# A fused attention and MLP kernel on one core: hand-written instruction order replaced by a list schedule with a timing model

## The chip, the cores and the metric

The kernel runs on one core of one Trainium2 chip. The metric is device time in microseconds (us) of one execution, lower is better. Runs of one kernel mostly agree within about 1%; times below are medians of runs in the fast state, also where record and table of a kernel include a slow one. Engines are named as in the profile: PE is TensorE, PEld its weight loads, DVE is VectorE, ACT is ScalarE, POOL is GpSimd, SP is the queue that issues most transfers.

## The reference

Squared-ReLU attention without softmax, followed by a squared-ReLU MLP. Inputs and output are float32.

```python
batch, n_heads, seq, head_dim = (8, 12, 448, 64)     # q, k, v
n_tokens, d_model, d_ff = (3584, 768, 2048)          # w_in, w_out

scores = scale * np.matmul(q, k.transpose(0, 1, 3, 2))
attn = np.maximum(scores, 0.0) ** 2 / S
attn_out = np.matmul(attn, v)
x = attn_out.transpose(0, 2, 1, 3).reshape(B * S, H * D)
h = x @ w_in
r = np.maximum(h, 0.0)
out = (r * r) @ w_out
```

## The kernel before

All matmuls are fp16. PE has five kinds of work. Scores go to `sp` and attention times values to `avt`, both as groups of four 64x64 matmuls. The first layer goes to `hps`. The second layer goes to `ops`; most of it is a seven-product scheme in place of eight, which needs sums of activations that DVE makes into `comb`. Twelve transposes of q and k are the fifth kind.

Squared ReLU is done in two halves on two engines. For scores, DVE takes the maximum and ACT squares, or ACT takes the ReLU and POOL multiplies. For the first layer, ACT squares and DVE multiplies by the mask `x > 0`:

```python
def relu2(ps, dst, scale):
    nc.scalar.activation(out=dst, in_=ps, func=AF.Square, scale=scale)
    nc.vector.scalar_tensor_tensor(
        out=dst, in0=ps, scalar=0.0, in1=dst, op0=ALU.is_gt, op1=ALU.mult)

def by_sbuf(ps, dst, r, scale, first):
    if first is nc.vector:
        nc.vector.tensor_scalar_max(r, ps, 0.0)
        return lambda: nc.scalar.activation(out=dst, in_=r, func=AF.Square, scale=scale)
    nc.scalar.activation(out=r, in_=ps, func=AF.Relu, scale=scale)
    return lambda: nc.gpsimd.tensor_mul(dst, r, r)
```

The order on every engine is the order in which the program calls these. After a start of its own, the program goes in "bursts": two tiles of scores, their squared ReLU, perhaps the 28 matmuls of attention times values, then a share of dense work (first and second layer) from a queue:

```python
def soft_burst(g, pool):
    todo = []
    for z, (n, t, sp) in enumerate(g):
        ...                                    # cut: buffers
        if z == 1 and not pool:
            relu2(ps, at, SK)
        else:
            todo.append(by_sbuf(ps, at, r, SK, nc.scalar if z else nc.vector))
    for fn in todo:
        fn()

for i in range(STREAM // 2, NB):
    ...                                        # cut: scores of two tiles into g
    soft_burst(g, not 22 < i <= 30)
    ...                                        # cut: attention x values, new dense work, loads
    run_some(max(0.0, (queued - KEEP) / (nxt - i)))     # dense work
```

Of the kernel before, what the change touches and what calls it, by code (L numbers as in the profile page):

```python
# [12 lines left out]
ALU = mybir.AluOpType  # L13


@with_exitstack
def kernel(
# [23 lines left out]
    NF = FF // P  # L41
    HALF = DM // 2
# [5 lines left out]
    ctx.enter_context(tc.manual_schedule())  # L48

    const_p = ctx.enter_context(tc.tile_pool(name="const", bufs=1))  # L50
    v_p = ctx.enter_context(tc.tile_pool(name="vp", bufs=4))
    raw_p = ctx.enter_context(tc.tile_pool(name="rawp", bufs=2))
    blk_p = ctx.enter_context(tc.tile_pool(name="blkp", bufs=2))
    qkt_p = ctx.enter_context(tc.tile_pool(name="qktp", bufs=3))
    at_p = ctx.enter_context(tc.tile_pool(name="atp", bufs=12))
    x_p = ctx.enter_context(tc.tile_pool(name="xp", bufs=2))
    g_p = ctx.enter_context(tc.tile_pool(name="gp", bufs=2))
    rest_p = ctx.enter_context(tc.tile_pool(name="restp", bufs=2))
    comb_p = ctx.enter_context(tc.tile_pool(name="combp", bufs=6))
    part_p = ctx.enter_context(tc.tile_pool(name="partp", bufs=6))  # L60
    rel_p = ctx.enter_context(tc.tile_pool(name="widep", bufs=2))

    PSUM = bass.MemoryType.PSUM
    s_p = ctx.enter_context(tc.tile_pool(name="sps", bufs=2, space=PSUM))
    mm_p = ctx.enter_context(tc.tile_pool(name="mmps", bufs=4, space=PSUM))






    raw: dict = {}
    early: list = []
    blk: dict = {}
    qkt: dict = {}
    vst: dict = {}

    def load_qk(n, w, eng, gate=None):
        b, u = divmod(n, NU)
        if n in (1, 2):  # L80
            if not early:
                early.append(g_p.tile([P, 4, 2 * TJ * D], FP32, name="early", tag="g"))
            t = early[0][:, 2 * n - 2 + (w == "k")].rearrange("p (f x) -> p f x", f=2)
        else:
            t = raw_p.tile([P, 2, TJ * D], FP32, name=w + "f", tag=w + "f")
        if gate is not None:
            gate.memset(t[0:1, 0, 0:1], 0.0)
        src = q if w == "q" else k
        eng.dma_start(
            out=t,  # L90
            in_=src[b, 4 * u:4 * u + 4].rearrange(
                "(f e) (p t) d -> (e p) f (t d)", e=2, t=TJ))
        raw[n, w] = t

    def cast_qk(n, w, op):
        src = raw.pop((n, w))
        t = blk_p.tile([P, TJ, 2 * D], FP16, name=w + "s", tag=w + "s")
        op(t.rearrange("p t (f d) -> p f t d", f=2),
           src.rearrange("p f (t d) -> p f t d", d=D))
        blk[n, w] = t  # L100

    def turn_dma(n, w):
        t = qkt_p.tile([P, TJ, P], FP16, name=w + "T", tag=w + "T")
        nc.sync.dma_start_transpose(
            out=t, in_=blk.pop((n, w)).rearrange("p t c -> p (t c)"))
        qkt[n, w] = t

    def turn_pe(n, w, op):
        src = blk.pop((n, w))
        ps = mm_p.tile([P, TJ * P], FP16, name="tps", tag="mm")  # L110
        for t in range(TJ):
            nc.tensor.transpose(ps[:, t * P:(t + 1) * P], src[:, t, :], ident)
        t = qkt_p.tile([P, TJ, P], FP16, name=w + "T", tag=w + "T")
        op(t.rearrange("p t c -> p (t c)"), ps)
        qkt[n, w] = t

    def load_v(n):
        b, u = divmod(n, NU)
        t = vst[n] = v_p.tile([P, 2, TJ * D], FP16, name="vs", tag="vs")
        src = v[b].rearrange("(u x) (p t) d -> p u x (t d)", x=4, t=TJ)  # L120
        for r in range(2):
            hs = slice(1, 3) if r else slice(0, 4, 3)
            nc.gpsimd.dma_start(out=t[64 * r:64 * r + 64], in_=src[:, u, hs])  # L123

    w1 = [const_p.tile([P, NM, 512], FP16, name=f"w1_{i}", tag=f"w1_{i}") for i in range(4)]
    w2 = [[const_p.tile([P, NF // 2, HALF], FP16, name=f"w2_{hf}{i}", tag=f"w2_{hf}{i}")
           for i in range(2)] for hf in range(2)]

    def load_w1(i):
        nc.gpsimd.dma_start(  # L130
            out=w1[i],
            in_=moe_w_in[:, 512 * i:512 * (i + 1)].rearrange("(m p) f -> p m f", p=P))

    def load_w2(hf, i):
        nc.gpsimd.dma_start(
            out=w2[hf][i],
            in_=moe_w_out[1024 * i:1024 * (i + 1), hf * HALF:(hf + 1) * HALF].rearrange(
                "(f p) d -> p f d", p=P))

    NH = NF // 2  # L140
    LO, HI = slice(0, HALF), slice(HALF, DM)
    wt = [const_p.tile([P, NH, HALF], FP16, name=f"wt_{i}", tag=f"wt_{i}") for i in (1, 2, 4)]
    t1, t2, t4 = wt

    def combine_w2(k, eng):
        step, r = k // 2, slice(4 * (k % 2), 4 * (k % 2) + 4)
        (b11, b21), (b12, b22) = w2
        if step == 0:
            eng.tensor_sub(t1[:, r], b12[:, r], b11[:, r])
        elif step == 1:  # L150
            eng.tensor_sub(t2[:, r], b22[:, r], t1[:, r])
        elif step == 2:
            eng.tensor_sub(t4[:, r], t2[:, r], b21[:, r])
        else:
            eng.tensor_sub(b12[:, r], b22[:, r], b12[:, r])


    fifo: deque = deque()
    queued = 0.0
    xts: dict = {}  # L160
    gts: dict = {}
# [7 lines left out]
    credit = 0.0  # L169

    def run_some(ns):
        nonlocal queued, credit
        credit += ns
        while fifo and credit > 0:
            c, fn = fifo.popleft()
            fn()
            queued -= c
            credit -= c

    def relu2(ps, dst, scale):  # L180
        nc.scalar.activation(out=dst, in_=ps, func=AF.Square, scale=scale)  # L181
        nc.vector.scalar_tensor_tensor(  # L182
            out=dst, in0=ps, scalar=0.0, in1=dst, op0=ALU.is_gt, op1=ALU.mult)

    def by_sbuf(ps, dst, r, scale, first):

        if first is nc.vector:
            nc.vector.tensor_scalar_max(r, ps, 0.0)  # L188
            return lambda: nc.scalar.activation(out=dst, in_=r, func=AF.Square, scale=scale)  # L189
        nc.scalar.activation(out=r, in_=ps, func=AF.Relu, scale=scale)  # L190
        return lambda: nc.gpsimd.tensor_mul(dst, r, r)  # L191

    PARTS = slice(0, 4 * TP), slice(4 * TP, S)
    WHOLE = slice(0, S)

    def h_pair(f, cols):

        if 0 not in gts:
            gts[0] = g_p.tile([P, NF, S], FP16, name="g", tag="g")
        cell = [None]  # L200
        w = cols.stop - cols.start

        def half(z):
            def run():
                if z == 0:
                    cell[0] = mm_p.tile([P, 512], FP32, name="hps", tag="mm")
                for m in range(NM):
                    nc.tensor.matmul(  # L208
                        cell[0][:, z * w:z * w + w],
                        lhsT=w1[(f + z) // 4][:, m, (f + z) % 4 * P:((f + z) % 4 + 1) * P],  # L210
                        rhs=xts[0][:, m, cols], start=(m == 0), stop=(m == NM - 1),
                        skip_group_check=True)
                if z == 1:
                    relu2(cell[0][:, 0:2 * w].rearrange("p (f c) -> p f c", c=w),
                          gts[0][:, f:f + 2, cols], 1.0)
            return run

        return [(0.422 * w * NM, half(z)) for z in range(2)]

    def h_groups(b):  # L220
        gt = gts[b] = g_p.tile([P, NF, S], FP16, name="g", tag="g")
        xt = xts[b]

        def group(f):
            def run():
                hps = mm_p.tile([P, 512], FP32, name="hps", tag="mm")
                for m in range(NM):
                    nc.tensor.matmul(  # L228
                        hps[:, 0:S],
                        lhsT=w1[f // 4][:, m, (f % 4) * P:(f % 4 + 1) * P],  # L230
                        rhs=xt[:, m, :], start=(m == 0), stop=(m == NM - 1))
                relu2(hps[:, 0:S], gt[:, f, :], 1.0)
            return run

        return [(189.0 * NM, group(f)) for f in range(NF)]

    def store(places, cols, osb):
        for i, (b, t) in enumerate(places):
            nc.sync.dma_start(
                out=out[b * S:(b + 1) * S, cols].rearrange(  # L240
                    "(p t) d -> p t d", t=TJ)[:, t, :],
                in_=osb[64 * i:64 * i + 64])
# [178 lines left out]





    ats: dict = {}

# [271 lines left out]
```

## Time and profile before

| | before |
|---|---|
| time, median of 2 runs | 441.63 us (440.77 to 442.5) |
| span of the profiled run, mean granted clock | 436.3 us, 0.976 |
| all matmuls at the pace of runs without a wait | 344.3 us |
| steps between 64x64 and 128x128 work (176 of about 95 ns) | 16.6 us |
| PE not getting on ("stalls"): before 80 us, 80 to 380 us, after | 28.8, 39.1, 1.1 us |

Rows three to five are worked out from the start times of the matmuls in the trace. Within an undisturbed run a 448-column matmul starts 189 ns after the one in front of it, a 384-column one 163 ns, a round of four 64x64 ones about 188 ns; what two starts lie further apart, less 95 ns where the size of the array tile changes, is counted as a stall, in the stretch in which it begins. Start and tail are the other 6.5 us. Half-clock time is inside the stalls: about 20 us of the span have half the clock, so at most about 10 us of the stalls are due to it.

The page of the kernel before gives each engine's busy time, its share of the span and its instructions, and, further down, the chain of work that ended last by engine:

```profile
PE 388.4 (89%) x3264; PEld 204.4 (47%) x3264; DVE 272.7 (63%) x367; ACT 253.1 (58%) x383; POOL 231.1 (53%) x200
...
PE 53%; DVE 24%; ACT 16%; issue 6%; POOL 0%; DVEq 0%; ACTq 0%
```

PE is nearly always busy by this count, and yet only 53% of the chain runs over PE: for 40% of the span it was DVE or ACT that set the time. The view of waits of before says who waited for whom (total us, times, longest); these are lines on DVE, ACT and PE:

```profile
DVE g L182 <- ACT g L181: 94.1, 86, 2.5
ACT at L189 <- DVE rel L188: 78.0, 67, 6.2
...
PE sp L438 <- DVE rel L188: 9.3, 10, 2.9
...
PE avt L494 <- DVE g L182: 5.3, 10, 1.0
```

The first two lines together are a loop between ACT and DVE. The timeline of before shows one turn of it (start, us, engine, line, operation, and in brackets the idle time in front and who ended it):

```profile
285.44 3.58 PE L228 MATMUL hps<-xt,w 128*128 128x448 f16 x18
...
286.09 0.92 ACT L190 ACTIVATE rel<-sp 128x896 f32<-128x896 f32 x1
...
286.87 1.08 DVE L188 TENSOR_SCALAR rel<-sp 128x896 f32<-128x896 f32 x1
...
287.99 0.95 ACT L189 ACTIVATE at<-rel 128x896 f16<-128x896 f32 x1 [0.98 <-DVE rel L188]
288.84 1.39 ACT L181 ACTIVATE g<-hps 128x448 f16<-128x448 f32 x3
...
289.40 1.69 DVE L182 SCALAR_TENSOR_TENSOR g<-hps,g 128x448 f16<-128x448 f32 x3 [1.45 <-ACT g L181]
290.08 0.35 PE L494 MATMUL avt<-at,vs 64*64 64x448 f16 x1 [0.56 <-DVE g L182]
...
291.00 1.08 DVE L188 TENSOR_SCALAR rel<-sp 128x896 f32<-128x896 f32 x1
```

Three groups of six first-layer matmuls start at 285.44 us; at 189 ns each the first group is through at about 286.6. ACT could square it from 287.01 on, but the next operation in ACT's queue is the square `at`, whose input DVE finishes only at 287.95. ACT stands 0.98 us with work behind it that is ready. So the three squares of `g` come at 288.84, DVE stands 1.45 us in front of the masks, PE runs out of buffers and waits, and the next `rel` on DVE comes late, after which the loop begins again. The Trainium skill (TensorE: Matmul & The Clock Gate, section "Architectural detail: the array is 16× 32×32, not 1× 128×128") says that "ACT/DVE are strict FIFO"; the trace agrees in this place. It is not so in each of the 67 waits of the second line above. In the trace, a 448-column square of the first layer follows the start of its sixth matmul by 0.39 us at the least; by this measure such a square was ready behind the waiting score square in 26 of the 67 waits, for 18 of the 78.0 us. In the other waits no such square was held up.

### The profile page before, as it was taken

The numbers are of one execution on the slowest core, as the hardware profiler recorded it, in microseconds if no ns is written. First come the engines' busy times: TensorE is split into PE (matmuls) and PEld (weight loads), VectorE is DVE, ScalarE is ACT, GpSimd is POOL, SyncE is SP. The second block draws the span as 40 slices with busy tenths as digits, with TensorE's granted clock in tenths as the row PEclk, the third lists the DMA queues.
The fourth block names the chain that finished last, engine by engine and source line by source line (L and its number), as shares of the span: only waits on it lengthen the run. The fifth ranks groups of instructions, "written<-read, shape, count | busy, mean of one in ns | idle before, by whom it ended". The sixth has DMA issues, their size and how long they took to land.

```text
span 436.3 us, 8172 instructions
## 1 busy us (share of the span) xinstructions
PE 388.4 (89%) x3264; PEld 204.4 (47%) x3264; DVE 272.7 (63%) x367; ACT 253.1 (58%) x383; POOL 231.1 (53%) x200
## 2 busy tenths in 40 slices
PE   7688887899889999999899899997769997999995
PEld 3455655444445444444454444543434443555563
DVE  4756556378985558565875765764596654645642
ACT  3676578667645775577457476666526675434121
POOL 4768367999935575476746465564275433200100
PEclk9869989999989999999999999999998999999999
DMA  8999995886066464686176274656053200220143
GB/s 276 171 260 226 252 220 90 231 201 144 0 147 133 126 113 116 154 165 155 31 201 153 59 168 71 162 137 148 8 111 80 54 2 2 72 56 0 46 97 75
DMA packets 69669, 53.61 MB, mean 123 GB/s; under 512 B 36864, under 2 KB 69632, under 8 KB 69632
## 3 DMA queue, kind: packets, MB, share of 16 engines
q1 hardware_dynamic: 55152, 40.84, 36.3%
q0 software_dynamic: 14208, 11.80, 18.2%
q8 instruction: 25, 0.41, 0.4%
q10 hardware_dynamic: 272, 0.46, 0.3%
q14 instruction: 12, 0.10, 0.1%
HBM read 45.61 MB, written 11.01 MB: 130 GB/s over the span
## 4 chain that ended last, share of the span: by engine, by line
PE 53%; DVE 24%; ACT 16%; issue 6%; POOL 0%; DVEq 0%; ACTq 0%
PE ops L302 23%; PE hps L228 15%; DVE rel L188 11%; ACT at L189 8%; DVE g L182 6%; ACT g L181 5%; PE avt L494 5%; PE sp L438 4%; DVE comb L283 4%; PE ops L266 2%; PE hps L208 2%; PE warm L565 1%; ACT xt L509 1%; DVE osb L313 1%; ACT rel L190 1%
## 5 line engine op out<-in xcount | busy, mean ns | idle before, releaser
L191 POOL TENSOR_TENSOR at<-rel 128x896 f16<-128x896 f32 (+2 forms) x70 | 118.5, 1693 | 141.2 <-ACT rel L190 140.8
L228 PE MATMUL hps<-xt,w 128*128 128x448 f16 x672 | 136.4, 353 | 7.9 <-DVE g L182 4.4
L182 DVE SCALAR_TENSOR_TENSOR g<-hps,g 128x448 f16<-128x448 f32 (+2 forms) x128 | 76.5, 621 | 94.3 <-ACT g L181 94.1
L189 ACT ACTIVATE at<-rel 128x896 f16<-128x896 f32 (+4 forms) x91 | 85.7, 943 | 78.6 <-DVE rel L188 78.0
L188 DVE TENSOR_SCALAR rel<-sp 128x896 f32<-128x896 f32 (+4 forms) x91 | 97.5, 1073 | 16.9 <-PE sp L438 14.8
L228 PEld LDWEIGHTS <-w 128*128 128x128 f16 x672 | 62.9, 98 | 75.8 <-issue 22.4
L181 ACT ACTIVATE g<-hps 128x448 f16<-128x448 f32 (+2 forms) x128 | 65.1, 537 | 32.4 <-PE hps L228 28.2
L190 ACT ACTIVATE rel<-sp 128x896 f32<-128x896 f32 (+2 forms) x70 | 64.1, 915 | 16.4 <-PE sp L438 15.0
L438 PE MATMUL sp<-qT,kT 64*64 64x448 f16 (+2 forms) x756 | 53.6, 349 | 15.2 <-DVE rel L188 9.3
L302 PEld LDWEIGHTS <-comb 128*128 128x128 f16 x416 | 40.1, 100 | 40.3 <-issue 9.6
L494 PE MATMUL avt<-at,vs 64*64 64x448 f16 (+2 forms) x756 | 45.0, 338 | 10.0 <-DVE g L182 5.3
L313 DVE SCALAR_TENSOR_TENSOR osb<-ops,part 128x384 f32<-128x384 f32 x52 | 28.6, 553 | 37.6 <-ACT part L308 30.7
L308 ACT ACTIVATE part<-ops 128x384 f32<-128x384 f32 x52 | 24.8, 486 | 34.6 <-PE ops L302 33.7
L302 PE MATMUL ops<-wt,comb 128*128 128x384 f16 x208 | 38.5, 337 | 4.9 <-DVE comb L283 4.7
L302 PE MATMUL ops<-w,comb 128*128 128x384 f16 x208 | 38.0, 334 | 2.0 <-ACT part L308 2.0
L438 PEld LDWEIGHTS <-kT 64*64 64x64 f16 x756 | 17.2, 107 | 45.0 <-issue 43.6
L494 PEld LDWEIGHTS <-vs 64*64 64x64 f16 x756 | 25.2, 109 | 24.5 <-issue 17.5
L302 PEld LDWEIGHTS <-g 128*128 128x128 f16 x264 | 25.3, 98 | 18.9 <-issue 2.5
L302 PE MATMUL ops<-w,g 128*128 128x384 f16 x176 | 30.9, 326 | 0.0
L123 POOL DMA_DIRECT2D vs<-in_v_dram x48 | 30.0, 630 | 0.1
L283 DVE TENSOR_TENSOR comb<-g 128x1024 f16<-128x1024 f16 x22 | 25.9, 1176 | 0.1
L208 PE MATMUL hps<-xt,w 128*128 128x256 f16 (+1 forms) x192 | 24.7, 278 | 0.8 <-DVE g L182 0.4
(49 smaller groups left out, 255.2 us busy)
## 6 DMA issues: line engine op xcount, KB each, us to landing
out_dram<-osb SPq DMA_DIRECT2D x112, 96.0 KB, 2.2
kf<-in_k_dram SPq DMA_DIRECT2D x22, 448.0 KB, 4.1
qf<-in_q_dram SPq DMA_DIRECT2D x21, 448.0 KB, 4.8
vs<-in_v_dram POOLq DMA_DIRECT2D x48, 112.0 KB, 3.1
w<-in_moe_w_in_dram POOLq DMA_DIRECT2D x4, 768.0 KB, 15.7
w<-in_moe_w_out_dram POOLq DMA_DIRECT2D x4, 768.0 KB, 18.2
early<-in_k_dram SPq DMA_DIRECT2D x2, 448.0 KB, 7.2
early<-in_q_dram SPq DMA_DIRECT2D x2, 448.0 KB, 8.1
```

Of the source, the lines that this page charges most:

```text
L181: nc.scalar.activation(out=dst, in_=ps, func=AF.Square, scale=scale)
L182: nc.vector.scalar_tensor_tensor(out=dst, in0=ps, scalar=0.0, in1=dst, op0=ALU.is_gt, op1=ALU.mult)
L188: nc.vector.tensor_scalar_max(r, ps, 0.0)
L189: return lambda: nc.scalar.activation(out=dst, in_=r, func=AF.Square, scale=scale)
L190: nc.scalar.activation(out=r, in_=ps, func=AF.Relu, scale=scale)
L191: return lambda: nc.gpsimd.tensor_mul(dst, r, r)
L208: nc.tensor.matmul(cell[0][:, z * w:z * w + w], lhsT=w1[(f + z) // 4][:, m, (f + z) % 4 * P:((f + z) % 4 + 1) * P], rhs=xts[0][:, m, cols] ...
L228: nc.tensor.matmul(hps[:, 0:S], lhsT=w1[f // 4][:, m, (f % 4) * P:(f % 4 + 1) * P], rhs=xt[:, m, :], start=(m == 0), stop=(m == NM - 1))
L283: op(t, x, y)
L302: nc.tensor.matmul(st[bank][:, 0:HALF], lhsT=st[a][:, j, :], rhs=w(j), start=(first and j == 0), stop=(j == NH - 1), skip_group_check=True)
L438: nc.tensor.matmul(sp[64 * c:64 * c + 64, e, at:at + w].rearrange("p (t c) -> p t c", c=TP), lhsT=kT[r, t, 64 * e:64 * e + 64], rhs=qT[r, ...
L494: nc.tensor.matmul(ap[f][64 * e:64 * e + 64, at0:at0 + w], lhsT=vs[r, e ^ c, t * D:(t + 1) * D], rhs=at[r, e, :], start=(t == 0), stop=(t ...
```

## The change

The intent is to let a small simulation choose the order. While the program is built, every operation is added to a `Plan` with its duration, its inputs, its buffers and a due time. An event loop then plays the program: whenever an engine is free it takes, of the operations that are ready and have buffers, the one with the earliest due time. The engine of an elementwise operation can be left open (ACT or DVE, ACT or POOL), and the buffer is whichever is free. What the loop issues is emitted in that order; the result is a fixed program, nothing is decided on the chip. The number of matmuls and the transfers are as before, and so is the arithmetic, except that eight score tiles which were squared and then masked are now treated like the others. Buffers that were bound to one use or engine are now drawn from common pools. The core of the diff:

```diff
+class Plan:
+    LAG = {"PE": 0.22, "ACT": 0.07, "DVE": 0.07, "POOL": 0.1, "SP": 0.0}
+    SWITCH = {("dense", "tile"): 0.09, ("tile", "dense"): 0.235}
...
+    def run(self):
...
+            now = heapq.heappop(events)
...
+                for eng in ("PE", "ACT", "DVE", "POOL", "SP"):
+                    if self.busy[eng] > now + 1e-9:
+                        continue
+                    got = self.pick(eng, now, waiting)
...
+                    op.end = begin + took
+                    self.busy[eng] = begin + busy
...
+                    emit()
...
+    def pick(self, eng, now, waiting):
+        for z, (_, _, op) in enumerate(waiting):       # sorted by due time
+            if op.ready > now + 1e-9:
+                continue
+            for alt in op.alts:
+                if alt[0] != eng:
+                    continue
+                if len(alt) > 5 and self.busy["POOL"] > now + 0.4 and op.due > now:
+                    continue
...                                                     # cut: are buffers free?
+                    return z, alt
...
+    def square(op, sp, width, pool="at"):
...
+        first = plan.add([
+            dve(n, lambda: nc.vector.tensor_scalar(...)),
+            act(n, lambda: nc.scalar.activation(...))],
+            [op], [sp, r], due=plan.now + 0.2)
+        second = plan.add([
+            act(n, lambda: nc.scalar.activation(out=dst(), in_=rel(), func=AF.Square)),
+            ("POOL", 0.0018 * n + 0.05, 0.0018 * n + 0.08,
+             lambda: nc.gpsimd.tensor_mul(dst(), rel(), rel()))],
+            [first], [r, at], due=plan.now + 4.0)
...
-        soft_burst(g, not 22 < i <= 30)
...
+            second, at = square(op, sp, S)
...
+    plan.run()
```

## The prediction

> **What bounds the kernel now.** TensorE. The page gives PE 89% busy, DVE 63%, ACT 58%, POOL 53%. From the start times of matmuls I get the pace inside a run without waits: 189 ns per 448-column matmul of the first layer, 163 ns per 384-column matmul of the second, about 188 ns per round of four 64x64 matmuls. At that pace all matmuls together need about 344 us. Steps between 64x64 and 128x128 work cost about 95 ns each over the pace, 176 times: 17 us. Start and tail are 6.5 us. The rest of the 436.3 us span, about 69 us, is PE not getting on: 29 us before 80 us, 39 us from 80 to 380 us, 1 us after that (the chain of waits there is matmuls alone). About 10 us of the 69 are clock: the granted clock is 0.976 on average, with half-clock stretches mostly before 68 us, some at 132 and 337 us. The Trainium skill (TensorE: Matmul & The Clock Gate, Part 1) describes a half-rate state after idle windows; the records agree (only 1.0 and 0.5 occur).
>
> The waits name the cause: score matmuls wait for DVE or ACT to empty the two score buffers (19 big gaps, about 18 us by starts), attention-value matmuls, 21 gaps, 14 us, first layer 22, 13 us, second layer 24, 10 us. No engine that serves PE is full. These are order losses: in the chain, PE stands behind `rel` (11%) and `at` (8%) while dense work is ready but later in its fixed order. DVE sums (`comb`) take 0.68 us undisturbed, 1.1 on average and once 5.0 us with POOL active at the same time (window 312 to 332 us: PE waited 2.9 us after that).
>
> **What the change does.** The arithmetic, matmul count, shapes and stores stay. PE floor 344 us and the number of mode steps stay about the same. Moved: PE takes the earliest-due ready operation; evacuations go to whichever of ACT, DVE, POOL the model finds free (rel 1.08 us on DVE or 0.92 on ACT, square 0.95 on ACT or 1.69 on POOL); sums wait for a quiet POOL and are placed 7 us ahead. Elementwise work (DVE 273, ACT 253, POOL 231 us) fits easily under 400 us. Its constants (0.1892, 0.1625, 0.00081 and 0.001045 us per element, 3.06 us POOL subtraction) match this trace. Costs: order is still static, so wrong times become head-of-line waits; SP queue order mixes loads, transposes and stores.
>
> **Sum (estimates from the numbers above).** 80 to 380 us: of 35 us of stalls other than clock, a little over half goes, -20. Before 80 us: DMA is 80 to 90% busy there and clock is cold, so only -6. Tail 0; mode steps +2. About -24 us.
>
> Predicted 417 us, 80% range 402 to 434. Faster by over 2%: 0.72; within: 0.17; slower: 0.11.
>
> **Checks in the profile.** PE busy share rises to about 93%; matmul sum unchanged; stalls by starts fall from 69 to about 45 us; waits of scores on `rel` shrink most; `comb` mean falls toward 0.7 to 0.8 us; POOL/ACT/DVE busy totals within 10%; the first 80 us shorten by about 6 us; PE mode steps about 176.
>
> **What would make it wrong.** Model time drifting from chip time, so that engines block on operations placed too early; POOL and DVE colliding more; loads or transposes queued late behind stores on SP; greedy PE order multiplying mode steps; the first 80 us limited by transfers.

## The result, and the profile after

After takes 397.24 us (median of 2 runs, 396.36 to 398.11) against 441.63 us. The ratio is 0.8995, with a 95% interval of 0.8881 to 0.9109. A ratio is the mean time of one kernel's fast runs over that of the other's fast runs of the same rounds, so it is not quite the ratio of the medians. The prediction said faster, which was right, but 417 us with a range from 402, which was not: the gain is 44 us, not 24.

| | before | after |
|---|---|---|
| profiled span, clock | 436.3 us, 0.976 | 396.3 us, 0.983 |
| matmuls at their pace | 344.3 us | 344.1 us |
| steps between 64x64 and 128x128 work | 176, 16.6 us | 184, 17.3 us |
| stalls before 80 us | 28.8 us | 20.5 us |
| stalls 80 to 380 us | 39.1 us | 7.8 us |
| stalls after 380 us | 1.1 us | 0.0 us |

The sum of the differences is the whole of the 40 us between the two spans: the stalls went, and little else moved. (The profiled run of before was the fastest of its kind, 438.1 us, that of after the slower of two, hence 40 rather than 44.) The page of after, the same two lines:

```profile
PE 377.3 (95%) x3264; PEld 200.3 (51%) x3264; DVE 264.7 (67%) x364; ACT 268.8 (68%) x392; POOL 222.4 (56%) x194
...
PE 80%; DVE 7%; POOL 4%; DMA 3%; ACT 3%; issue 2%; SPq 0%; DVEq 0%; POOLq 0%; ACTq 0%
```

The chain now runs over PE for 80% of the span. The waits of after (line numbers differ: L456 is the mask, L461 the first-layer square, L381 the score square on ACT, L383 that on POOL, L374 the maximum on DVE, L348 the scores):

```profile
POOL at L383 <- DVE rel L374: 75.3, 35, 6.6
DVE g L456 <- ACT g L461: 48.9, 67, 2.2
...
ACT at L381 <- DVE rel L374: 5.5, 6, 2.3
...
PE sp L348 <- DVE rel L374: 2.1, 4, 1.0
```

The wait of the score square on ACT fell from 78.0 to 5.5 us, that of the mask from 94.1 to 48.9. A part of the first fall is only a change of engine: POOL now squares tiles that DVE emptied, which before was left to ACT, and has the wait for them (75.3 us). The timeline of after, in a stretch like the one above:

```profile
228.77 0.57 PE L348 MATMUL sp<-qkt,qkt 64*64 64x448 f16 x8
228.88 0.54 ACT L461 ACTIVATE g<-mm 128x448 f16<-128x448 f32 x1 [0.64 <-PE mm L472]
...
229.28 2.44 PE L472 MATMUL mm<-xt,w 128*128 128x448 f16 x12
229.32 0.91 ACT L377 ACTIVATE rel<-sp 128x896 f32<-128x896 f32 x1
229.47 1.09 DVE L374 TENSOR_SCALAR rel<-sp 128x896 f32<-128x896 f32 x1 [1.29 <-PE sp L348]
230.26 0.95 ACT L381 ACTIVATE at<-rel 128x896 f16<-128x896 f32 x1
230.48 0.61 DVE L456 SCALAR_TENSOR_TENSOR g<-mm,g 128x448 f16<-128x448 f32 x1
230.64 1.68 POOL L383 TENSOR_TENSOR at<-rel 128x896 f16<-128x896 f32 x1 [0.76 <-DVE rel L374]
```

ACT, DVE and POOL wait here only for something that PE or DVE has just made, and PE has no wait at all.

The start is different. The first score matmul began at 8.07 us before and begins at 12.20 us after. In the timeline of after, DVE at the start:

```profile
8.50 0.62 DVE L291 COPY qkt<-mm 128x896 f16<-128x896 f16 x1 [7.35 <-PE mm L288]
...
9.04 0.62 DVE L271 CAST blk<-raw 128x896 f16<-128x896 f32 x1
```

The cast at 9.04 is that of the very first q, which ACT loads; before, its cast began at 5.80. The plan lets ACT issue that load only at 2.6 us and so reckons that it lands at 10.0 us, after both loads of the next unit, and puts a copy for that unit in front of it.

### The profile page after: what moved, and what is told of

The parts are those of the page before. It is cut to its first block, busy times and chain, and to the rows that moved or that the text cites. A ratio compares the mean times of both kernels' runs of the same rounds, so it can differ in the third digit from the quotient of the medians.

```text
span 396.3 us, 8280 instructions
## 1 busy us (share of the span) xinstructions
PE 377.3 (95%) x3264; PEld 200.3 (51%) x3264; DVE 264.7 (67%) x364; ACT 268.8 (68%) x392; POOL 222.4 (56%) x194
## 4 chain that ended last, share of the span: by engine, by line
PE 80%; DVE 7%; POOL 4%; DMA 3%; ACT 3%; issue 2%; SPq 0%; DVEq 0%; POOLq 0%; ACTq 0%
PE mm L472 34%; PE mm L623 26%; PE sp L348 9%; PE mm L411 8%; DVE comb L602 3%; PE mm L561 3%; DVE rel L374 2%; DMA g<-in_q_dram 2%; POOL at L383 2%; DMA raw<-in_q_dram 1%; POOL blk L271 1%; DVE g L456 1%; PE mm L288 1%; ACT rel L377 1%; POOL wt L587 1%
## 5 line engine op out<-in xcount | busy, mean ns | idle before, releaser
L472 PE MATMUL mm<-xt,w 128*128 128x448 f16 (+2 forms) x864 | 157.3, 332 | 0.3 <-DVE g L456 0.3
L383 POOL TENSOR_TENSOR at<-rel 128x896 f16<-128x896 f32 (+1 forms) x60 | 102.3, 1705 | 86.7 <-DVE rel L374 75.3
L374 DVE TENSOR_SCALAR rel<-sp 128x896 f32<-128x896 f32 (+2 forms) x88 | 94.2, 1073 | 36.8 <-PE sp L348 29.3
L456 DVE SCALAR_TENSOR_TENSOR g<-mm,g 128x448 f16<-128x448 f32 (+2 forms) x128 | 79.2, 620 | 49.3 <-ACT g L461 48.9
L461 ACT ACTIVATE g<-mm 128x448 f16<-128x448 f32 (+2 forms) x128 | 68.9, 541 | 45.7 <-PE mm L472 44.0
L381 ACT ACTIVATE at<-rel 128x896 f16<-128x896 f32 (+2 forms) x98 | 91.1, 940 | 9.2 <-DVE rel L374 5.5
L348 PE MATMUL sp<-qkt,qkt 64*64 64x448 f16 (+2 forms) x756 | 52.4, 353 | 4.7 <-DVE rel L374 2.1
L271 POOL CAST blk<-raw 128x896 f16<-128x896 f32 x42 | 39.8, 957 | 22.3 <-issue 7.7
L545 ACT ACTIVATE part<-mm 128x384 f32<-128x384 f32 x48 | 23.5, 489 | 41.0 <-PE mm L623 38.9
L623 PE MATMUL mm<-wt,comb 128*128 128x384 f16 x208 | 37.0, 327 | 1.4 <-DVE comb L602 1.4
L411 PE MATMUL mm<-at,vs 64*64 64x448 f16 (+1 forms) x672 | 37.3, 339 | 0.4 <-POOL at L383 0.4
L623 PEld LDWEIGHTS <-g 128*128 128x128 f16 x264 | 24.8, 98 | 20.1 <-issue 4.3
L348 PEld LDWEIGHTS <-qkt 64*64 64x64 f16 x756 | 17.3, 110 | 30.8 <-issue 30.2
L317 POOL DMA_DIRECT2D vs<-in_v_dram x48 | 30.1, 633 | 0.1
```

What stands on the lines that cost most here:

```text
L271: return lambda: fn(blk.tile.rearrange("p t (f d) -> p f t d", f=2), tile_of().rearrange("p f (t d) -> p f t d", d=D))
L317: nc.gpsimd.dma_start(out=buf.tile[64 * r:64 * r + 64], in_=src[:, u, hs])
L348: nc.tensor.matmul(sp[64 * c:64 * c + 64, e, c0:c0 + w].rearrange("p (t c) -> p t c", c=TP), lhsT=kT[r, t, 64 * e:64 * e + 64], rhs=qT[r, ...
L374: dve(n, lambda: nc.vector.tensor_scalar(out=rel(), in0=sp.tile[:, :, 0:width], scalar1=0.0, scalar2=SK, op0=ALU.max, op1=ALU.mult)),
L381: act(n, lambda: nc.scalar.activation(out=dst(), in_=rel(), func=AF.Square)),
L383: lambda: nc.gpsimd.tensor_mul(dst(), rel(), rel()))],
```

## The experiments

Four rival causes were set up: A, PE passes over an operation that is not ready; B, the free choice of engine; C, the order of the helper engines ACT, DVE and POOL (or the buffers); D, the times in the plan, that is, whether the order needs them to be right. Stalls are worked out as in the tables above, from one profiled run of each. In fixed_engines and wrong_short one stall of 6 us, PE waiting for a square on POOL, begins just before 80 us and ends after it, and is counted before. Twelve kernels ran; all gave correct results. "Before" took 441.2 to 442.3 us (median) in the three sessions.

| kernel | median us of the fast runs | ratio to before | stalls 0 to 80, 80 to 380 us |
|---|---|---|---|
| before | 441.6 | 1 | 28.8, 39.1 |
| after | 397.2 | 0.900 | 20.5, 7.8 |
| start_order | 413.0 | 0.934 | 27.1, 18.3 |
| pe_in_order | 421.1 | 0.953 | profile slow |
| fixed_engines | 403.8 | 0.914 | 23.5, 11.2 |
| both_fixed | 416.2 | 0.942 | 27.2, 17.5 |
| loads_first | 395.5 | 0.896 | 21.0, 7.0 |
| early_squares | 398.1 | 0.903 | 20.2, 7.7 |
| no_clock | 487.3 | 1.106 | 32.1, 71.7 |
| before_late_squares | 418.0 | 0.947 | 26.6, 22.4 |
| pe_in_order_2 | 422.4 | 0.958 | 30.1, 21.1 |
| fixed_engines_2 | 396.5 | 0.899 | 16.6, 7.0 |
| wrong_each | 400.7 | 0.909 | 20.1, 13.4 |
| wrong_short | 419.7 | 0.954 | 29.3, 19.3 |

### First session: the start, and one part at a time

**start_order.** The start looked like a mistake that was easy to mend.

```diff
-        eng, name = (nc.scalar, "ACT") if (n, w) == (0, "q") else (nc.sync, "SP")
+        eng, name = (nc.scalar, "SP") if (n, w) == (0, "q") else (nc.sync, "SP")
```

> The kernel after, with one word changed: the plan counts the first q load on the SP queue beside the k load instead of on ACT (it is still issued from ACT). In the trace of after, DVE waited 7.35 us for a transpose of unit 1 while the q of unit 0 lay ready, and the first score matmul began at 12.2 us, against 8.1 us before the change. Theory that the start is an error of the plan's load times: first scores at about 8.1 us, time about 3 to 4 us below the 397.2 of after, near 394. Rival that transfers or helper engines bound the first 40 us anyway: first scores early, but the time stays at 396 to 398.

Measured: 413.0 us, 16 us slower than after; both theories missed. The timeline of GpSimd in start_order shows it: the first weight loads are issued at 21.08 us (14.48 in after), behind squares of scores, and later GpSimd stands in its load issues:

```profile
32.18 0.88 POOL L327 DMA_DIRECT2D w<-in_moe_w_out_dram  x1 [0.15 <-issue]
39.48 0.60 POOL L317 DMA_DIRECT2D vs<-in_v_dram  x1 [6.43 <-DMA w<-in_moe_w_in_dram]
44.47 0.60 POOL L317 DMA_DIRECT2D vs<-in_v_dram  x1 [4.39 <-DMA w<-in_moe_w_in_dram]
48.08 0.89 POOL L327 DMA_DIRECT2D w<-in_moe_w_out_dram  x1 [3.00 <-DMA w<-in_moe_w_in_dram]
```

The view of PE's waits in start_order begins with those weights:

```profile
PE mm L472 <- DMA w<-in_moe_w_in_dram: 6.5, 2, 3.9
```

Why: the due time of a load is worked back from its user by a fixed 7.1 us (`took = 7.0` in the whole kernel), which is less than the time until it has landed, 13.0 us in the median in after. With scores ready earlier, squares beat the loads. What exactly holds the next load issue until a weight load has landed was not separated. An order can be spoilt by a transfer that is only a little late, and the sound start of after was partly luck.

**pe_in_order.** As start_order, and PE may only take the first operation of its own line:

```diff
+        self.line = deque(op for op in self.ops if op.alts[0][0] == "PE")
+        self.line.append(None)
...
+            if eng == "PE" and op is not self.line[0]:
+                continue
```

> As start_order, but TensorE must take its operations in the order in which they were added (the order of the kernel before); engine choice and the order of ACT, DVE and POOL still by the plan. Theory A, that the gain comes from TensorE passing over an operation that is not ready: most of the gain goes, 420 to 435 us, stalls between 80 and 380 us back near 30 us. Theory B, engine choice, or C, the order of the helper engines and the buffers: within 5 us of start_order.

Measured: 421.1 us in its fast runs, 8 us over start_order. The order in which operations are added follows the same bursts as the hand order, but is not the same sequence of matmuls throughout. The run stands on a spoilt start, so it says little. It was measured again, below.

**fixed_engines.** As start_order, and each elementwise operation has only the engine that it had before. The main lines:

```diff
-        first = plan.add([ dve(...), act(...) ], [op], [sp, r], due=plan.now + 0.2)
+        first = plan.add(firsts[onact:onact + 1], [op], [sp, r], due=plan.now + 0.2)
-        second = plan.add([ act(...), ("POOL", ...) ], [first], [r, at], due=plan.now + 4.0)
+        second = plan.add(seconds[onact:onact + 1], [first], [r, at], due=plan.now + 4.0)
```

> As start_order, but every elementwise operation is on the engine that the kernel before used (in bursts 23 to 30 both tiles go DVE then ACT); TensorE order and all other orders by the plan. Theory A or C: within 5 us of start_order. Theory B, engine choice: 410 us or more, and ACT and DVE busy totals back to 253 and 273.

Measured: 403.8 us, faster than start_order. With few squares on POOL the weight loads went out from 13.2 us on. So B cannot be a large part, but again the start is mixed in.

**both_fixed.** Both limits.

> As start_order with both limits: TensorE in the order added and engines as before; only the order on ACT, DVE and POOL, the loads and the buffers come from the plan. Theory A: as pe_in_order, 420 to 435 us. Theory B: as fixed_engines. Theory C (helper order and buffers): below 410 us although both other parts are gone. If it is near 440, nothing is left for C.

Measured: 416.2 us. Though PE keeps the hand order and the engines are those of before, 26 of the 44 us are there. That speaks for theory C: what is left of the plan is mainly the order of the helper engines, the loads and the buffers. The expected line "below 410" was missed by 6 us.

### Second session: the order of the helpers

**before_late_squares.** If C is the loop shown above, it can be opened in the kernel before, without any plan: emit the score squares after half of the burst's dense work.

```diff
-        for fn in todo:
-            fn()
+        return todo
...
-        soft_burst(g, not 22 < i <= 30)
+        seconds = soft_burst(g, not 22 < i <= 30)
...
-        run_some(max(0.0, (queued - KEEP) / (nxt - i)))
+        some = max(0.0, (queued - KEEP) / (nxt - i))
+        run_some(some / 2)
+        for fn in seconds:
+            fn()
+        run_some(some / 2)
```

> The kernel before with one thing moved: the second halves of the score work (squares on ScalarE and GpSimd) are emitted after half of the dense work of the same burst instead of before it. Theory C1 (ScalarE standing in a score square): 420 to 430 us, stalls between 80 and 380 us from 39 to below 28 us. If C1 is wrong: 436 to 446 us.

Measured: 418.0 us, as expected. Seven lines put into the hand-written kernel, and four taken out, bring 23 of the 44 us. The sequence of matmuls in the two traces is the same. In the view of waits of before_late_squares the wait that is meant is less than a third of the 78.0 of before:

```profile
DVE g L182 <- ACT g L181: 70.4, 93, 2.1
...
ACT at L189 <- DVE rel L188: 23.0, 19, 5.7
```

By the measure used above, not one of these 19 waits has a ready first-layer square behind it (26 of 67 in before). Stalls between 80 and 380 us fell from 39.1 to 22.4. New buffers are not needed for this: C, as far as these 23 us go, is the order of the helpers. The edit moves the multiplies of POOL too; the squares of ACT alone were not tried.

**early_squares.** The opposite, in after: give the squares the priority that makes them come first.

```diff
-            [first], [r, at], due=plan.now + 4.0)
+            [first], [r, at], due=plan.now + 0.25)
```

> The kernel after with one number changed: a square of scores is due 0.25 us after its score matmul instead of 4.0 us, so that ScalarE takes it ahead of first-layer squares. both_fixed (416.2) showed that most of the gain stays without TensorE order and engine choice, so it is in the order of the helper engines (theory C) or in buffers. Theory C1, that the loss of before was ScalarE standing in a score square that waits for VectorE while first-layer squares, and VectorE's masks behind them, wait: 405 to 420 us, stalls between 80 and 380 us from 7 to 20 us or more. Rival (priorities matter little once the plan knows what is ready, since it never lets an engine stand in front of an operation that is not ready): 395 to 401.

Measured: 398.1 us, stalls between 80 and 380 us 7.7 us. C1 in the form "low priority of the square" falls, the rival holds: the plan, by its own times, never puts an engine in front of an operation that is not ready, and then the priority hardly matters. The harm in before was not that the square comes first, but that it comes before its input.

**no_clock.** The engines of before, the graph, the due times and the buffers of after, but no times: operations are emitted by due time as soon as their inputs have been emitted.

```diff
-        events = sorted({0.0} | {op.after for op in self.ops} | set(self.busy.values()))
...                                             # cut: the whole event loop
         while done < n_ops:
+            for z, (_, _, op) in enumerate(waiting):
...                                             # cut: are buffers free?
+                    break
...
+            op.alts[0][3]()
+            done += 1
```

> fixed_engines (403.8) without any timing: the operations are emitted by due time as soon as their inputs were emitted and buffers are free in the order of emission; no durations, no readiness. Theory T, that knowing when an operation is ready is what gains: 430 us or more, near before. Rival P, that the priorities and the buffers suffice: within 8 us of both_fixed, 408 to 424.

Measured: 487.3 us, 46 us slower than before and 71 us slower than both_fixed, which comes nearest to it; 71.7 us of stalls between 80 and 380 us. Theory T holds. But half of the 46 us is a single stall of 23.4 us: PE waits for a mask, the mask for a square on ACT, the square for a copy on POOL, and POOL had stood idle 6.3, 6.2 and 6.6 us in front of casts of q and k before it came to that copy. So the direction is shown, and the size hangs on one such chain. The same graph and due times without times are worse than the hand order, which had its look-ahead tuned.

**loads_first.** start_order, with the four first weight loads in front.

```diff
-                "(m p) f -> p m f", p=P)), WQ)], after=after)
+                "(m p) f -> p m f", p=P)), WQ)], after=after, due=after - 2.0)
```

> start_order, with the four loads of the first weights given a due time 2 us before their start time, so that GpSimd issues them ahead of squares. In start_order the first weight load was issued at 21.1 us (14.5 in after), its matmuls waited 6.5 us for it, and GpSimd then stood 13.8 us in all in three load issues. Theory that the loss of start_order (413 against 397) is these late loads and what follows from them: weights issued by 13 to 18 us, no wait for them, first scores at about 8 us, time 392 to 396. Rival that an early start only moves the wait to the transfers: 398 to 413.

Measured: 395.5 us (393.3 to 396.9, ratio 0.8963, interval 0.8915 to 0.9011). The loss of start_order is gone, so the late loads were its cause. It is the fastest median, but its interval lies inside that of after, so it is not shown to be faster. The stalls before 80 us did not fall below those of after (21.0 and 20.5 us, one profile each): what the early start gains is waited for later.

### Third session: clean parts, and wrong times

**pe_in_order_2.** PE held to its order again, now on loads_first; the edit is that of pe_in_order.

> loads_first (395.5, sound start) with TensorE held to the order in which its operations were added. The first try of this (421.2) stood on start_order, whose start was spoilt, so the part is measured again. If passing over blocked operations is worth what the pair both_fixed and fixed_engines showed (12 us): 404 to 412, stalls between 80 and 380 us from 7 to about 17 us. If it is worth most of the gain (theory A): over 415. If nothing: under 398.

Measured: 422.4 us, 27 us over loads_first. This is theory A's figure, and yet before_late_squares showed that 23 us come from the helpers alone. Both are true: with PE in the order added, three quite different helper orders (both_fixed, before_late_squares, this one) all end between 416 and 422 us. Set free, PE comes down to 395. A part of the 27 us is clock: the mean granted clock was 0.972 here and 0.990 in loads_first, which is at most about 8 us (an estimate from these shares and the spans). In the plan of after, as it is built, 78 of the 410 groups of PE work are issued while one that was added earlier still waits. The timeline of PE in pe_in_order_2 shows what it then waits for:

```profile
288.20 1.31 PE L478 MATMUL mm<-xt,w 128*128 128x448 f16 x6
290.06 1.30 PE L478 MATMUL mm<-xt,w 128*128 128x448 f16 x6 [0.56 <-DVE g L462]
```

**fixed_engines_2.** The engines of before, on loads_first; the edit is that of fixed_engines.

> loads_first with every elementwise operation on the engine of the kernel before. Theory B (the choice of engine gains): over 405. If the choice is worth little, as fixed_engines (403.8, with late weight loads of 17 to 21 us landing) suggested: 395 to 401.

Measured: 396.5 us, the same as loads_first. Theory B falls: choosing the engine per operation, the most visible part of the change, is worth nothing here that these runs can see. Its view of waits also shows that the wait of ACT on `rel` is no measure of the time by itself: it is 18.2 us, near the 23.0 of before_late_squares, which takes 21 us longer.

```profile
ACT at L383 <- DVE rel L376: 18.2, 30, 2.2
```

**wrong_each.** loads_first, with wrong durations in the plan for every elementwise operation except the sums:

```diff
+                    if eng in ("ACT", "DVE", "POOL") and not rest:
+                        wrong = 0.6 + 0.8 * (op.id * 7919 % 1000) / 999
+                        busy, took = busy * wrong, took * wrong
```

> loads_first, but the plan reckons every elementwise operation with a duration that is wrong by a factor between 0.6 and 1.4, other for each. In the trace of after the plan's durations are right to 1% in the median and its start times drift by 5 us at most over the run. My prediction took half of the gain off for drift. If the exact times are what makes the order good: 410 to 430 us, stalls between 80 and 380 us above 20 us. If an order made with rough times does as well: 394 to 402.

Measured: 400.7 us in three fast runs (398.1 to 402.7), 5 us over loads_first. The fourth run (404.6) was counted as slow, being over 1.5% above the fastest; its granted clock, 0.982, was not low. With it the median is 401.7. The intervals of the two ratios just overlap (0.9004 to 0.917 and 0.8915 to 0.9011), so the loss is small and not sharply measured: errors of up to 40% in both directions cost about a tenth of the gain.

**wrong_short.** All elementwise durations but those of the sums at 0.6:

```diff
+                    if eng in ("ACT", "DVE", "POOL") and not rest:
+                        busy, took = 0.6 * busy, 0.6 * took
```

> loads_first, but the plan reckons all elementwise operations at 0.6 of their time, so that it thinks every result ready too early and puts operations in front of ones that could run, as the hand order did. If exact times matter: 410 to 430 us, more than wrong_each, since the error has one direction. If not: 394 to 402.

Measured: 419.7 us, 24 us over loads_first, and this though PE may still pass over. The waits of wrong_short show the DVE half of the loop again (79.3 us, after loads_first's 49.4). POOL waits longer for `rel` (89.8 us, after 73.1), once 12.1 us, and PE waits for POOL:

```profile
POOL at L385 <- DVE rel L376: 89.8, 30, 12.1
DVE g L458 <- ACT g L463: 79.3, 99, 2.5
...
PE mm L413 <- POOL at L385: 7.5, 3, 5.9
```

## Why the prediction was right or wrong

- **What bounds the kernel: right.** PE, with about 344 us of matmuls, 17 us of steps, and stalls. The Trainium skill (TensorEngine Tiling (Array Packing), "Key Properties") says that changing the tiling mode drains TensorE; the traces agree, at about 95 ns a step, 176 steps before and 184 after. The forecast "+2 us" for them was +0.7.
- **That the stalls are losses of order: right, but half of the order was not in it.** The prediction names dense work that stands later in PE's fixed order, the choice of engine and the place of the sums. It does not name the order on the helper engines, and before_late_squares gains 23 us by that alone, with PE's sequence unchanged.
- **The term that was wrong: "of 35 us of stalls other than clock, a little over half goes, -20".** Stalls between 80 and 380 us fell by 31 us, to 7.8. Half-clock records account for at most 3.4 us of before's, and after has none in that stretch, so the term itself measured about -28. All stalls together fell from 69 to 28 us, where about 45 was forecast. (The half-clock stretches that the prediction puts at 132 and 337 us are counted from the start of the trace; in the span they begin at 122.0 and 326.8 us.)
- **Why it was mis-sized.** I took off nearly half because "order is still static, so wrong times become head-of-line waits". The premise is true and the size of the error was not looked at. Set against the trace of after, operation by operation in each engine's order, the plan's durations on DVE are right to 0.5% in the median (80% of them between 0.99 and 1.01), those on ACT too (0.96 to 1.04), and its start times are between 2.9 us early and about 5 us late over the whole run. wrong_each shows that errors of up to 40% without a common direction would have cost about 5 us. Of the errors tried, only times that are all too short bring the result that I forecast: wrong_short, 419.7 us. The prediction had noted that the constants match the trace, and did not draw the conclusion. How much of the missing 8 us comes from this and how much from the helper order that it left out was not separated.
- **The first 80 us: right in size, by another course.** Predicted -6, measured -8.3, in spite of a first score that came 4 us later, which was not foreseen; that the size fits is partly luck.
- **Waits of scores on `rel` shrink most: right in the view of waits (9.3 to 2.1 us), but only a small part.** Most of the stalls that went were in front of other matmuls, which fits a loop that also keeps the banks of the first layer from coming free.
- **`comb` mean falls to 0.7 or 0.8 us: wrong.** It went from 1.02 to 0.99 us, and 18 of 52 sums still took over 0.75 us (16 before). The step that failed is a reading of the code: the lead of 7 us belongs to the loads; a sum is due only 0.8 us before its user, and the plan keeps it from a busy POOL only until it is due. 45 of the 52 sums were overdue when the plan placed them, and it reckoned 17 of them at over 0.75 us itself, with a mean of 0.94. The Trainium skill (GPSIMD Engine Reference, "1. Specifications") says that GpSimd shares its SBUF interfaces with DVE instructions that have two SBUF inputs, as these sums have; the traces agree with that: the 16 slow sums of before (up to 5.03 us) and the 18 of after all overlap an instruction on POOL, and of the 25 and 26 sums that overlap none, each took at most 0.75 us (11 and 8 more overlap one and are as fast). No run here removed POOL's work to test it. PE's wait for sums was 2.1 us after, so slow sums cost little.
- **Other checks: right.** PE 95% (about 93 forecast); ACT +6%, DVE -3%, POOL -4% busy, all within 10%.
- **Engine choice** was listed among what moves, without a size; fixed_engines_2 gives it none.

What the parts are worth: opening the loop alone gives 418; with PE still in its hand order the plan's helpers give 416 to 422; both free give 395 to 397. The parts were not shown to add up in any other order: a free PE with the helpers as they were before was not run, because the hand order cannot be kept on one engine when another departs from it. The common pools of buffers were not tested by themselves either.

## What to carry to other kernels

When PE is the bound and every helper engine still has a third of its time free, look for an engine that stands in front of an operation whose input is late while ready work waits behind it; here, moving that one operation back brought half of what the full scheduler brings. A static order from a timing model held on the chip with durations that fit the trace; here random errors of up to 40% did little harm, durations that were all too short did much, and leaving time out was worse than a tuned hand order. Give loads a due time that counts until they land, not one with too short a lead, or a better start elsewhere will push them back.

## What the Trainium skill lacked or had wrong

- TensorE: Matmul & The Clock Gate says that the records show only the half and the full rate, beside 13/16 with several busy cores; it also warns that records can be unreliable and that the clock was seen stuck at a quarter. None of these is 0.555: one of the four runs of pe_in_order had a granted clock of 0.555 for most of its 641.6 us (0.5 in nearly all the rest), mean 0.556, on one core, and its length bears the low rate out; the other three ran at 420.1 to 421.3 us. What set it off is not known.
- TensorEngine Tiling (Array Packing) says that a change of mode drains the array and gives no figure: about 95 ns a step between 64x64 and 128x128 work, over 176 and 184 steps.
- No page that was read gives a way to judge how far a static order may be off. Here durations were right to 1% in the median over 396 us and the order drifted by 5 us; wrong by 0.6 to 1.4 at random cost about 5 us, by 0.6 throughout 24 us.
